# Issuing the first weight load ahead of the entry barrier, in a decode-attention kernel

## The chip, the cores and the metric

The kernel runs on one core of one Trainium2 chip. Time is device microseconds (us) of one execution; a result is the median of several executions. A profile (trace) of one execution comes with each kernel. Its "span" runs from the first to the last instruction. The engines go by the profile's short names: here PE runs the matmuls, DVE and ACT the copies, casts and activations, POOL (GpSimd) the fills of constants, and SP (SyncE) issues the large loads. A DMA is a transfer between device memory and the core's own; the profile counts 16 DMA engines.

## The reference, cut to what matters

Two attention blocks, A and B, each decode one token. A attends to the last 2048 positions of its cache, B to all 8192. Each block projects x with wq, attends over 16 key/value heads, and projects back with wo.

```python
B, Sq, D = 1, 1, 576
Hq, Hkv, Sk, Dh = 32, 16, 8192, 128          # bf16 everywhere
q = (x @ wq).reshape(B, Sq, Hq, Dh)...
scores = einsum(q, k) * Dh ** -0.5            # k: last 2048 rows (A), all 8192 rows (B)
o = einsum(softmax(scores), v)
out = concat([o_A @ wo_A, o_B @ wo_B])
```

All bytes are used once: 102.8 MB come from HBM (device memory), 2.3 KB go back.

## The kernel before

All large loads go through one queue, issued by SyncE (called SP) in a fixed order: A's wq (2, 2 and 0.5 MB), B's wq (the same), then k, v and wo. A load into a buffer that is still in use waits on SyncE for that use to end. ACT issues the two small loads of x.

```python
def load(dst, src, writes, dma, after=()):
    add("sp", lambda sp: sp.dma_start(dst, src()), writes=writes, dma=dma, after=after)

def load_x(P):
    def go(act):
        ...
            src = bass.AP(tensor=x.tensor, offset=x.offset, ap=[[9, 64], [4, 2], [1, 5]])
            return act.dma_start(xtwo[:, P, 0:5], src)
    add("act", go, writes=[("xtwo", P)], dma="x%d" % P)
...
for P in range(2):
    x_columns(P)
    parts = [(0, 4, vslots[:, 2 * P, :], ("v", 2 * P)), (1, 4, vslots[:, 2 * P + 1, :], ("v", 2 * P + 1)),
             (2, 1, kslots[:, 3, P * WQ_U:(P + 1) * WQ_U], ("k", 3, P))]
    for k, n, view, res in parts:
        load_wq(P, k, view, n, res)
        q_part(P, k, n, view, res)
    q_finish(P)
```

The list of recorded operations is then written out, engine by engine, into a block:

```python
def emit(self):
    ...
    per = {e: [o for o in self.ops if o.eng == e] for e in self.ENGINES}
    ...
    with self.nc.Block() as block:
        @block.sync
        def _(sp):
            run("sp", sp)
        ...
```

Ahead of that block stands an entry sequence that the kernel's author did not write. GpSimd fills four constants with memsets. Then all five engines meet in a barrier: each engine executes a Drain that raises a "gather" semaphore, and waits on a "release" semaphore, which GpSimd raises when the four others and its own Drain are through.

```
GpSimd: Memset x4, Drain, wait gather >= 4, release += 4
SyncE:  Drain (gather += 1), wait release >= 1       # ACT, PE and DVE likewise
```

Of the kernel before, what the change touches and what calls it, by code (L numbers as in the profile page):

```python
# [38 lines left out]
class Program:  # L39
# [147 lines left out]
    def emit(self):  # L187
        self.number()
        self.wants()
        per = {e: [o for o in self.ops if o.eng == e] for e in self.ENGINES}  # L190

        def one(eng, op):
            ins = op.fn(eng)
            if op.value is not None:
                ins.then_inc(self.sem(op.key), op.inc)

        def plain(eng, ops):
            for op in ops:
                for key in sorted(op.left, key=str):
                    eng.wait_ge(self.sem(key), op.left[key][1])  # L200
                one(eng, op)

        def looped(eng, ops):
            waits, before = self.waits_of_loop(ops)
            for key, n in sorted(before.items(), key=str):
                eng.sem_inc(self.sem(key), n)
            body = {}
            for o in ops:
                body.setdefault(o.loop[1], o)

            def some(todo):
                for place in todo:
                    for key, (n, take) in sorted(waits.get(place, {}).items(), key=lambda w: (not w[1][1], str(w[0]))):
                        ins = eng.wait_ge(self.sem(key), n)  # L214
                        if take:
                            ins.then_inc(self.sem(key), -n)
                    one(eng, body[place])

            def parts(of, i):
                todo = sorted(p for p in body if body[p].loop[3] == of)  # L220
                while todo:
                    cond = body[todo[0]].loop[2]
                    n = next((k for k, p in enumerate(todo) if body[p].loop[2] is not cond), len(todo))
                    if cond is None:
                        some(todo[:n])
                    else:
                        with eng.If(cond(i)):
                            some(todo[:n])
                    todo = todo[n:]

            with eng.Fori(0, self.outer) as v:
                with eng.Fori(*self.rounds_of(v)) as g:
                    parts("inner", g)
                parts("outer", v)

        def run(name, eng):
            ops = per[name]
            inside = [k for k, o in enumerate(ops) if o.loop]
            if not inside:
                plain(eng, ops)  # L240
                return
            lo, hi = inside[0], inside[-1] + 1
            assert len(inside) == hi - lo
            plain(eng, ops[:lo])
            looped(eng, ops[lo:hi])
            plain(eng, ops[hi:])

        with self.nc.Block() as block:
            @block.sync
            def _(sp):  # L250
                run("sp", sp)

            @block.gpsimd
            def _(pool):
                run("pool", pool)

            @block.tensor
            def _(pe):
                run("pe", pe)

            @block.vector
            def _(dve):
                run("dve", dve)

            @block.scalar
            def _(act):
                run("act", act)
# [488 lines left out]
```

## Time and profile before

| | before |
|---|---|
| time, median of 3 (range) | 250.03 us (249.70 to 250.04) |
| span of the profiled execution | 247.7 us |
| bytes loaded | 102.8 MB, nearly all through one queue, whose packets keep the 16 DMA engines busy for 98.0% of the span |
| PE, ACT, DVE busy | 68%, 35%, 33% |

The next lines are from the profile's page of the kernel before: the span, the mean busy share of the 16 DMA engines in 40 equal slices (in tenths), the rate in GB/s of each slice, and SyncE's queue.

```profile
span 247.7 us, 7505 instructions
...
DMA  7999999999999999999999999999999999999993
GB/s 270 406 433 431 430 431 421 426 423 429 431 425 429 426 421 431 422 431 434 423 429 429 423 431 429 426 437 426 429 429 423 431 426 429 434 427 427 421 406 138
...
q1 hardware_dynamic: 7936, 102.77, 98.0%
```

By the busy share only the first and the last slice are not full. The Trainium skill, "DMA: Bandwidth & Descriptors", section Specifications, gives 435 GB/s as the fabric's ceiling; most slices move 421 to 437 GB/s, so the trace agrees. Nothing that PE, ACT or DVE does can shorten such a kernel, as long as the queue is never empty. What can shorten it is an earlier start of the queue, a shorter tail after it, or fewer bytes.

The timeline shows the start. Its columns are start, duration (both us), engine, source line, operation. An engine's name with a q (SPq, ACTq) means its sequencer, which issues the DMAs; `x2` means two instructions merged into one row.

```profile
0.24 0.10 POOL L741 MEMSET const-float32-0.0<- 128x1 f32 x1 [0.24 <-issue]
...
0.34 0.10 POOL L741 MEMSET const-uint8-127<- 128x1 uint8 x1
0.73 0.60 ACTq L344 DMA_DIRECT2D xtwo<-in_A_x_dram  x1
...
0.73 0.86 SPq L380 DMA_DIRECT2D vslots<-in_A_wq_dram  x2
```

SyncE issues nothing until 0.73 us. The trace's finer records, not all of which the timeline prints, say why. SyncE's Drain stands at 0.000 us (it opens the span). GpSimd's memsets and its Drain last until 0.49 us. SyncE's wait for the release ends at 0.67 us. The first load's issue lasts from 0.734 to 1.123 us, and the first data packet starts at 1.745 us.

The same start by windows of time (columns: window, length, busy time of five engines, granted TensorE clock, DMA share, GB/s). A packet is booked whole in the window in which it begins, so the share can exceed 1 in a short window.

```profile
0.00:1.00 1.00, 0.00 (x0) 0.00 (x0) 0.00 (x0) 0.00 (x0) 0.47 (x6) 1.00 0.00 0
1.00:2.00 1.00, 0.00 (x0) 0.00 (x0) 0.00 (x0) 0.00 (x0) 1.00 (x5) 1.00 1.03 213
2.00:3.00 1.00, 0.00 (x0) 0.00 (x0) 0.00 (x0) 0.98 (x1) 1.00 (x6) 1.00 0.24 82
```

And the end, from the chain of work that ended last (start, duration, what):

```profile
220.75 23.73 DMA vslots<-in_B_wo_dram
244.48 0.04 issue
244.52 0.71 PE ktps L646 x12
245.23 0.02 issue
245.26 0.31 DVE outsb L652
```

This wo load was issued some 24 us ahead of its landing: it stood in the queue. (It is the last but one. The last, of 144 KB, landed 0.37 us after it; "the last wo load" means the one that the chain names.) After it come a last product, a cast, and the store of the output.

### The profile page before, as it was taken

How to read it: one execution, taken by the hardware profiler on the slowest of the kernel's cores; microseconds unless marked ns; L12 is line 12 of the kernel's file. 1: busy time of each engine (PE TensorE's matmuls, PEld its weight loads, DVE VectorE, ACT ScalarE, POOL GpSimd, SP SyncE). 2: the span in 40 equal slices, each digit the busy share in tenths (PEclk: the TensorE clock that was granted, in tenths of full speed). 3: DMA queues.
4: the chain of work that ended last, by engine and by line, in shares of the span. 5: the costliest groups of instructions: out<-in, count | busy, mean ns of one | idle time of the engine just before them, and what ended most of it. 6: DMA issues, size and time to landing. Idle time of an engine off the chain costs nothing. (4 is left out here: it accounts for less than half of the span.)

```text
span 247.7 us, 7505 instructions
## 1 busy us (share of the span) xinstructions
PE 169.6 (68%) x3406; PEld 132.3 (53%) x3406; DVE 81.0 (33%) x152; ACT 87.1 (35%) x92; POOL 12.9 (5%) x49
## 2 busy tenths in 40 slices
PE   0193589994999559995999638998345144685634
PEld 0031288763877458864878428785244142584522
DVE  0001225554555017564555122655004004204000
ACT  2000047767478009786578004775200000000000
POOL 7501000000000000000000000000000000000000
PEclk9999959999799979998899955999858755557555
DMA  7999999999999999999999999999999999999993
GB/s 270 406 433 431 430 431 421 426 423 429 431 425 429 426 421 431 422 431 434 423 429 429 423 431 429 426 437 426 429 429 423 431 426 429 434 427 427 421 406 138
DMA packets 8235, 102.92 MB, mean 416 GB/s; under 512 B 1184, under 2 KB 1312, under 8 KB 2080
## 3 DMA queue, kind: packets, MB, share of 16 engines
q1 hardware_dynamic: 7936, 102.77, 98.0%
q8 instruction: 8, 0.13, 0.2%
q10 hardware_dynamic: 288, 0.00, 0.1%
q14 instruction: 3, 0.02, 0.0%
HBM read 102.76 MB, written 0.00 MB: 415 GB/s over the span
## 5 line engine op out<-in xcount | busy, mean ns | idle before, releaser
L472 ACT ACTIVATE kt<-ktps 128x1024 bf16<-128x1024 bf16 x80 | 77.9, 1021 | 54.5 <-PE ktps L466 54.4
L466 PEld LDWEIGHTS ktps<-ident,kslots 128*128 128x128 bf16 x1280 | 78.9, 103 | 27.9 <-issue 27.9
L466 PE MATMUL ktps<-ident,kslots 128*128 128x128 bf16 x1280 | 85.1, 230 | 12.4 <-PEq L214 12.4
L475 DVE COPY kt<-ktps 128x1024 bf16<-128x1024 bf16 x80 | 55.2, 691 | 53.7 <-PE ktps L466 53.6
L557 PE MATMUL opsum<-vslots,ptm 128*32 128x128 bf16 x1280 | 28.1, 262 | 28.0 <-PEq L214 23.7
L557 PEld LDWEIGHTS opsum<-vslots,ptm 128*32 128x32 bf16 x1280 | 25.3, 119 | 31.6 <-issue 31.6
L486 PE MATMUL sacc<-kt,qst 128*32 128x512 bf16 x320 | 25.3, 392 | 1.8 <-PEq L214 1.8
L566 DVE TENSOR_TENSOR diag<-opsum,rows 128x512 f32<-128x512 f32 x5 | 3.5, 691 | 55.9 <-PE opsum L557 55.9
L425 PE MATMUL opsum<-vslots,xpad 128*32 128x512 bf16 x64 | 8.2, 489 | 14.8 <-DVE xpad L410 12.1
L599 ACT ACTIVATE stat<-stat 128x1 f32<-128x1 f32 (+1 forms) x2 | 0.6, 294 | 37.2 <-DVE stat L597 37.2
L425 PEld LDWEIGHTS opsum<-vslots,xpad 128*32 128x32 bf16 x64 | 2.3, 119 | 17.6 <-issue 13.1
L457 POOL COPY qst<-qtm 128x64 bf16<-128x64 bf16 x20 | 4.5, 236 | 123.2 <-PE sacc L486 113.5
L646 PE MATMUL ktps<-kslots,opj 128*32 128x144 bf16 x184 | 6.1, 326 | 5.8 <-DMA kslots<-in_B_wo_dram 3.9
L486 PEld LDWEIGHTS sacc<-kt,qst 128*32 128x32 bf16 x320 | 5.1, 94 | 8.2 <-issue 4.4
L431 ACT ACTIVATE qrow<-opsum 128x512 bf16<-128x512 f32 x2 | 1.2, 597 | 23.1 <-PE misc L425 23.1
L523 ACT ACTIVATE psb<-sacc,stat 128x2048 bf16<-128x2048 f32 x3 | 5.9, 1967 | 8.5 <-DVE stat L517 8.5
L646 PEld LDWEIGHTS ktps<-kslots,opj 128*32 128x32 bf16 x184 | 5.2, 145 | 6.4 <-DMA kslots<-in_B_wo_dram 4.2
L425 PE MATMUL misc<-vslots,xpad 128*32 128x512 bf16 x64 | 8.2, 487 | 0.0
L630 PE MATMUL misc<-acc,pick 128*128 128x32 f32 x16 | 3.8, 404 | 3.6 <-DVE acc L624 2.9
L433 DVE CAST qrow<-misc 128x512 bf16<-128x512 f32 x2 | 1.4, 692 | 14.6 <-PE misc L425 14.6
L652 DVE CAST outsb<-ktps 128x144 bf16<-128x144 f32 x2 | 0.6, 307 | 16.0 <-PE ktps L646 16.0
L630 PEld LDWEIGHTS misc<-acc,pick 128*128 128x128 f32 x16 | 3.6, 328 | 3.8 <-DVE acc L624 3.0
(66 smaller groups left out, 62.1 us busy)
## 6 DMA issues: line engine op xcount, KB each, us to landing
kslots<-in_B_k_cache_dram SPq DMA_DIRECT2D x16, 2048.0 KB, 19.6
vslots<-in_B_v_cache_dram SPq DMA_DIRECT2D x16, 2048.0 KB, 18.4
kslots<-in_A_k_cache_dram SPq DMA_DIRECT2D x4, 2048.0 KB, 29.8
vslots<-in_A_v_cache_dram SPq DMA_DIRECT2D x4, 2048.0 KB, 23.5
vslots<-in_A_wq_dram SPq DMA_DIRECT2D x2, 2048.0 KB, 9.9
vslots<-in_B_wq_dram SPq DMA_DIRECT2D x2, 2048.0 KB, 19.6
kslots<-in_A_wo_dram SPq DMA_DIRECT2D x2, 2016.0 KB, 23.8
kslots<-in_B_wo_dram SPq DMA_DIRECT2D x1, 2016.0 KB, 31.2
```

The costliest lines, as they stand in the source:

```text
L425: ins = pe.matmul(qps[c][32 * j:32 * j + 32, :], lhsT=xpad[:, P, x, :], rhs=src[:, o:o + 512], start=(u == 0), stop=(u == WQ_UNITS - 1))
L433: add("dve", lambda dve: dve.tensor_copy(qrow[:, 512:1024], misc[:, :]), reads=[B_M], writes=[("qrow", 1)])
L457: add("pool", lambda pool: pool.tensor_copy(qst[:, s * 64:(s + 1) * 64], qtm[:, o:o + 64]), reads=[("qtm", KIND[g])], writes=[("qst", s)], ...
L466: ins = pe.matmul(ktps_bf[q][:, t * 128:(t + 1) * 128], lhsT=kslots[:, s, o:o + 128], rhs=ident[:, :], start=True, stop=True, is_transpose ...
L472: add("act", lambda act, q=q, dst=dst: act.activation(dst, ktps_bf[q], ACT.Copy), reads=[("bank", q)], writes=[("kt", u % NKT, q)], tag="e ...
L475: add("dve", lambda dve, q=q, dst=dst: dve.tensor_copy(dst, ktps_bf[q]), reads=[("bank", q)], writes=[("kt", u % NKT, q)], tag="e%d%d" % ( ...
L486: ins = pe.matmul(sacc[32 * j:32 * j + 32, 512 * half:512 * half + 512], lhsT=qst[:, s * 64 + e * 32:s * 64 + e * 32 + 32], rhs=rhs, start ...
L523: return act.activation(psb[:, :].rearrange("p (x g) -> p x g", g=2), src, ACT.Exp, bias=st(P, C_NB + k), scale=SCALE, accum_out=st(P, C_L ...
L557: ins = pe.matmul(opsum[32 * j:32 * j + 32, s * DH:(s + 1) * DH], lhsT=ptm[:, o:o + 32], rhs=vslots[:, s, b * 128:(b + 1) * 128], start=(u ...
L566: return dve.tensor_tensor(diag[:, g % 2, :, :], opsum[:, :].rearrange("p (s d) -> p d s", s=NS), m, ALU.mult)
L630: ins = pe.matmul(misc[:, 0:32], lhsT=pick[:, r, :], rhs=acc[:, d, 32 * r:32 * r + 32], start=(r == 0), stop=(r == 3))
L646: ins = pe.matmul(ktps[P][32 * j:32 * j + 32, 0:OUTW], lhsT=opj[:, P, jj:jj + 32], rhs=view[:, o:o + OUTW], start=(jj == 0), stop=(jj == H ...
```

## The change

The intent is to let the first 2 MB load start while the engines are still meeting at the barrier. It touches a buffer that nothing in the entry sequence touches, and waits for nothing.

```diff
+        first = per["sp"].pop(0)
+        assert not first.left and first.dma is not None
+        one(self.nc.sync, first)
+        lead = self.nc.cur_bb.bb.instructions
+        ins = lead.pop()
+        at = next(k for k, o in enumerate(lead) if o.engine == ins.engine and "Drain" in str(o))
+        lead.insert(at, ins)
+
         with self.nc.Block() as block:
```

The instruction is taken from the end of the entry sequence and put ahead of SyncE's Drain. No instruction and no byte is added or removed.

## The prediction

> **What bounds the kernel.** Its data transfers, almost from start to end. The page's DMA row reads 9 tenths in 38 of 40 slices, one SyncE queue holds 98% of the DMA time, and nearly all slices move 421 to 437 GB/s. The Trainium skill, "DMA: Bandwidth & Descriptors", section Specifications, gives a fabric ceiling of 435 GB/s; the trace agrees. In the packet records that queue has no stretch over 0.15 us with fewer than 12 packets in flight between 1.92 and 243.5 us. PE is busy 68%, ACT 35%, DVE 33%. The chain of waits ends with the last wo load (23.7 us, mostly queueing), then matmul 0.71 us, a cast 0.31 us, the output store. So the span is: first issue at 0.73 us, 1.0 us to the first data packet, 242 us of saturated transfer, a tail of 3.5 us.
>
> **What the change does.** It moves one instruction: SyncE's first load of A's wq (2 MB) goes ahead of SyncE's drain for the entry barrier. In the timeline the span starts with that drain at 0.00 us; SyncE waits for the others (GpSimd's four memsets, 0.24 to 0.44 us, and its drain, to 0.49 us), is released at 0.66 us, and issues its first load at 0.734 us, taking 0.389 us. The first packet starts at 1.745 us: 1.01 us after the issue began, 0.62 us after it ended. (Same page, section "Latency and other measured facts": about 0.6 us to the first byte; the trace agrees counted from the issue's end.) Nothing is added or removed; the load depends on nothing computed.
>
> **What it is worth.** The issue should begin near 0.00 us and the first packet near 1.0 us, 0.73 us earlier. The 2 MB keep the queue busy 4.9 us, and the second load is issued when the barrier opens (about 0.73 us), so no pause follows. As the queue is never empty, the 0.73 us should travel to the end whole: all of it is on the critical path.
>
> The barrier should not open later: SyncE's issue ends near 0.40 us, GpSimd's drain at 0.49 us: 0.1 us of slack. The x loads (issued at 0.73 us, landing at 10.9 us) may land as before; PE's first matmul (11.4 us) waits for them, but PE later waits for B's wq, so that is hidden.
>
> **Prediction.** 250.03 - 0.73 = 249.30; I allow 0.05 us of loss: 249.35 us, range 248.9 to 249.9. Faster by over 2%: 0.01; within 2%: 0.98; slower: 0.01. The runs of before spread over 0.34 us, half the gain.
>
> **What the profile would show if right.** SyncE's first issue near 0.0 us, before the barrier; the second near 0.73 us; first data packet near 1.0 us; the other engines' starts unchanged within 0.1 us; the page's first slice above 300 GB/s (before 270); every later load landing about 0.7 us earlier, wo's last too; the same tail; span near 247.0 us.
>
> **What would make it wrong.** (1) The first issue takes much longer, or its first packet waits for something that was ready by 1.7 us: less gain. (2) SyncE's drain waits for the transfer itself: barrier 5 us late, the second load too, slower by microseconds. (3) The clock that times the kernel starts with something that moves with the first issue: gain in the span, none in the time. (4) A pause elsewhere in the queue, set by PE's release of a slot, absorbs the head start: landings early at first, not at the end.

## The result

| | before | after |
|---|---|---|
| time, median of 5 (range) | 250.03 us (249.70 to 250.25) | 249.26 us (248.82 to 249.32) |
| ratio | | 0.9969 (95%: 0.9957 to 0.9981) |
| span of the profiled execution | 247.7 us | 247.5 us |

A ratio is the mean time of one kernel's runs over that of the other's runs of the same rounds, so it is not quite the ratio of the medians. By the means the gain is 0.79 us (249.98 to 249.19). It is a change of 0.3%, small, but its interval excludes 1.

The same lines of the page, for the changed kernel:

```profile
span 247.5 us, 7505 instructions
...
DMA  8999999999999999999999999999999999999992
GB/s 326 391 444 427 432 424 421 421 429 437 429 430 418 421 426 426 430 432 426 429 426 426 429 432 426 434 429 424 432 424 429 429 426 434 429 426 425 421 407 106
...
q1 hardware_dynamic: 7936, 102.77, 98.1%
```

The first slice moves 326 GB/s in place of 270; the middle is as it was. The timeline of the start:

```profile
0.00 1.13 SPq L388 DMA_DIRECT2D vslots<-in_A_wq_dram  x2
0.23 0.10 POOL L749 MEMSET const-float32-0.0<- 128x1 f32 x1 [0.23 <-issue]
...
0.33 0.10 POOL L749 MEMSET const-uint8-127<- 128x1 uint8 x1
...
0.79 0.61 ACTq L352 DMA_DIRECT2D xtwo<-in_A_x_dram  x1
```

The first issue starts at 0.00 us. (The 1.13 us merges two issues: the finer records have them at 0.000 and 0.793 us.) The barrier opens 0.05 us later than before. The windows show the queue's start moved up:

```profile
0.00:1.00 1.00, 0.00 (x0) 0.00 (x0) 0.00 (x0) 0.00 (x0) 0.42 (x6) 1.00 0.00 0
1.00:2.00 1.00, 0.00 (x0) 0.00 (x0) 0.00 (x0) 0.00 (x0) 1.00 (x4) 1.00 1.21 262
2.00:3.00 1.00, 0.00 (x0) 0.00 (x0) 0.00 (x0) 0.92 (x1) 1.00 (x6) 1.00 0.91 377
```

The first data packet starts at 1.002 us, 0.743 us earlier. So far all is as forecast. But the chain's end is not:

```profile
220.51 23.82 DMA vslots<-in_B_wo_dram
244.33 0.04 issue
244.38 0.71 PE ktps L654 x12
245.09 0.02 issue
245.11 0.31 DVE outsb L660
```

The last wo load lands at 244.33 us, against 244.48 us: 0.15 us earlier, not 0.74. These two profiles alone would say that four fifths of the head start were lost on the way, while the times say that all of it arrived. One of the two misleads, and the first experiments ask which.

### The profile page after: what moved, and what is told of

Read it like the earlier page. It is cut to its first block, busy times and chain, and to the rows that moved or that the text cites. A ratio compares the mean times of both kernels' runs of the same rounds, so it can differ in the third digit from the quotient of the medians.

```text
span 247.5 us, 7505 instructions
## 1 busy us (share of the span) xinstructions
PE 168.7 (68%) x3406; PEld 131.5 (53%) x3406; DVE 80.8 (33%) x152; ACT 87.2 (35%) x92; POOL 12.9 (5%) x49
```

## The experiments

Two theories stood after this.

- **Full queue.** The head start travels through a queue that is never empty, and arrives whole. The pair of profiles is unlucky.
- **Given back.** The head start is lost near the end of the queue, and the time was gained by something outside the span.

Nine runs were made, two of them repeats, all correct. Each was timed in 4 to 6 executions beside 9 to 11 executions of the kernel before on the same chip (three chips in all). "Over before" below is the difference of the means.

| run | time, median | ratio (95%) | over before |
|---|---|---|---|
| again_before | 249.93 us | 0.9995 (0.9983 to 1.0007) | -0.03 us |
| again_after | 249.26 us | 0.9971 (0.9958 to 0.9984) | -0.68 us |
| late_first | 252.86 us | 1.0120 (1.0105 to 1.0135) | +2.99 us |
| nine_ahead | 249.14 us | 0.9968 (0.9956 to 0.9980) | -0.83 us |
| late_both | 253.44 us | 1.0143 (1.0128 to 1.0157) | +3.56 us |
| x_ahead | 249.20 us | 0.9969 (0.9956 to 0.9982) | -0.75 us |
| split_plain | 250.07 us | 1.0006 (0.9993 to 1.0018) | +0.18 us |
| split_ahead | 249.73 us | 0.9992 (0.9979 to 1.0005) | -0.16 us |
| x_on_sp | 249.12 us | 0.9965 (0.9952 to 0.9979) | -0.86 us |

### again_before and again_after: the same two kernels once more

No edit. The point is to have the span of every execution, of both kernels on one chip.

> The kernel before, unchanged, run as if it were a new one: it gives the spans of its executions beside their times, which the first result lacks. Theory (the head start of 0.73 us travels through a queue that is never empty): time 250.0 us, ratio 1.000, spans near 247.7 us, so that the spans of the changed kernel are about 0.7 us shorter on average and the one profile that showed 0.14 us less was an unlucky one. Rival (the head start is given back at the end of the queue, and the time gained 0.77 us from something outside the span): time minus span stays near 2.4 us in every execution here, and near 1.8 us in the changed kernel, with spans that differ by 0.2 us only.

> The changed kernel again, on the same chip as the run above. Theory: time 249.3 us, ratio 0.997, mean span about 0.7 us below that of the unchanged kernel. Rival: time 249.3 us as well, but mean span only 0.1 to 0.3 us lower, and time minus span near 1.8 us against 2.4 us.

The mean span was 248.03 us for the kernel before (6 executions; 248.10 us over the 11 others in the same rounds) and 247.40 us for the changed kernel (5; the first result's five average 247.36 us). The spans differ by 0.6 to 0.7 us, as the times do, and time minus span is the same for both. The rival "given back" falls. The first profile of the kernel before, with 247.7 us, was shorter than nearly all of its other executions. The new profile of the same kernel ends its chain so:

```profile
221.47 23.74 DMA vslots<-in_B_wo_dram
245.21 0.04 issue
245.25 0.71 PE ktps L646 x11
245.96 0.02 issue
245.98 0.31 DVE outsb L652
```

Here the last wo load lands at 245.21 us, 0.73 us later than in the first profile of the same kernel. The packet records show what differs between executions of one kernel. From the first packet to the 102nd MB they took nearly the same time. From the 102nd MB to the last packet of the loads they did not:

| profile | first packet | to 102nd MB | to the last load packet | to the end |
|---|---|---|---|---|
| before, first profile | 1.75 us | +240.04 us | +2.66 us | +3.22 us |
| before, again_before | 1.74 us | +240.16 us | +3.21 us | +3.27 us |
| after, first profile | 1.00 us | +240.16 us | +3.15 us | +3.21 us |
| after, again_after | 1.00 us | +240.29 us | +2.97 us | +3.22 us |

The time to the last packet varies by half a microsecond from one execution to the next, as much as most of the effect under study. Only the first column differs by kernel, and it differs by 0.74 us. The spans of these profiles, paired each way, show gains from 0.14 to 0.9 us.

The last 0.8 MB only bring the difference to light; it arises much earlier. Each load reports 16 completions, one for each DMA engine, and has landed when the slowest engine is done. In all eleven traces the slowest engine fell behind the mean of the 16 by another 0.6 to 1.4 us between two loads that landed at 19 to 31 us, and more than half of its lag stayed to the end. How large it was near 140 us goes with the length of the tail (correlation 0.98). At the time of the jump the queue of kind "instruction" put its first 16 KB packet (1.0 to 1.2 us) among the loads; that it is the cause was not tested. Averaged over the 16 engines, the same wo load was done at 243.66 and 243.79 us before, and at 243.04 and 243.28 us after: earlier by 0.38 to 0.75 us in every pair.

### late_first: the same lever pulled the other way

If a start 0.73 us earlier is worth 0.73 us, a start 3.5 us later must cost 3.5 us, which is far above the noise. The edit, on the kernel before:

```diff
-        add("sp", lambda sp: sp.dma_start(dst, src()), writes=writes, dma=dma, after=after)
+        add("sp", lambda sp: sp.dma_start(dst, src()), reads=["ident"] if dma == "wq00" else (), writes=writes, dma=dma, after=after)
```

> The kernel before, with the first load made to wait until GpSimd has written the identity (about 4.2 us in the trace of before), so that the first issue starts near 4.2 us in place of 0.73 us, 3.5 us late. Theory (whatever the queue's start is late or early goes whole to the end): time 253.5 us, 3.5 us over before (3.2 to 3.8), and the last wo load lands 3.5 us later. Rival (the pipeline has room that absorbs part of a late or early start, for instance by waits of SyncE on PE): under 2.5 us over before.

The time rose by 2.99 us, between the two forecasts: a miss for the stated 3.2 to 3.8 us. The last wo load landed 3.3 us later than in the first profile of before and 2.6 us later than in the second, not 3.5. The first packet came at 5.216 us, 3.47 us late. From there to the 102nd MB it took 239.78 us, less than in any of the four profiles in the table above. Something in the start had become cheaper. The timeline of late_first shows a side effect of the edit: the x loads are still issued at once, into an empty queue.

```profile
0.74 0.61 ACTq L344 DMA_DIRECT2D xtwo<-in_A_x_dram  x1
1.38 0.62 ACTq L344 DMA_DIRECT2D xtwo<-in_B_x_dram  x1
...
4.21 0.86 SPq L380 DMA_DIRECT2D vslots<-in_A_wq_dram  x2
```

The view of the tile that x is loaded into has the time from issue to landing, for late_first:

```profile
DMA to landing us min/median/max: 2.1/2.1/2.2
```

In the kernel before the two x loads took 10.1 and 12.7 us, because their 288 tiny packets (10 bytes of data or a 4-byte semaphore write each) ran among the wq packets, from 5.4 to 13.7 us.

### late_both: is it the x packets that late_first saved?

Both x loads wait for the identity as well, so they are again issued together with the first wq load. The edit on late_first (the calls also move behind the identity's definition):

```diff
-        add("act", go, writes=[("xtwo", P)], dma="x%d" % P)
+        add("act", go, reads=["ident"], writes=[("xtwo", P)], dma="x%d" % P)
```

> As late_first, but the two x loads on ACT wait for the identity too, so that they are again issued with the first wq load and not 3.5 us ahead of it. It asks why late_first cost 2.9 us where its first packet came 3.47 us late. In late_first the x packets went through the empty queue from 2.1 to 3.2 us; in the kernel before they run from 5.3 to 14.0 us among the wq packets. Theory (x's 288 small packets, mixed with the wq packets, cost the bulk transfer some 0.4 us, and late_first saved that): about 3.5 us over before, 253.4 us, and the bulk takes as long from its first packet to its 102nd MB as in before (240.0 to 240.2 us). Rival (slack in the pipeline absorbed 0.5 us of the delay): 252.9 us as in late_first, with the bulk again 0.3 to 0.4 us shorter.

The time rose by 3.56 us, the first packet came 3.49 us late, and the bulk took 240.24 us from first packet to 102nd MB, as in before. The x loads took as long as ever to land:

```profile
DMA to landing us min/median/max: 10.2/11.5/12.8
```

So a late start goes whole to the end, and the shortfall of late_first was the x packets. Mixed with the wq packets, they lengthen the bulk by 0.26 to 0.51 us (the four profiles above against 239.78 us; 0.46 us from late_both; nine_ahead and x_ahead below, with 240.01 and 240.31 us, widen this to 0.22 to 0.53 us). All of these rest on the one profile of late_first. The mean times of late_first and late_both differ by 0.60 us; no execution of one reaches the range of the other (252.78 to 253.10 and 253.43 to 253.70 us), though the intervals of the ratios, from two chips, just overlap.

The records also show where the two part. Counted from the first packet, the 1st MB had come after 3.40 us in late_first and 3.43 in late_both, the 4th after 10.41 and 10.86 us, and this 0.45 us stays to the 102nd MB. The x packets of late_both ran from 3.6 to 12.0 us of the same count. From the 15th to the 102nd MB every one of the eleven traces took 203.56 to 203.66 us: apart from the tail, what differs between these kernels lies in the first 15 MB.

### nine_ahead: does the barrier itself matter?

All nine loads that wait for nothing go ahead of SyncE's Drain. The barrier then opens very late, for all engines.

```diff
-        first = per["sp"].pop(0)
+        for _ in range(9):
+            first = per["sp"].pop(0)
             ... (the rest of the moved block, indented)
```

> All nine loads that wait for nothing (both wq, three of A's k) are issued ahead of SyncE's drain, so the barrier opens only after some 4 to 5 us and every other engine starts that much later; x lands later, PE's first matmul starts near 15 us in place of 11.3 us. Theory (only the time of the first issue counts, the barrier and the other engines' starts are off the path): time 249.3 us as with one load ahead, within 0.3 us. Rival (a late barrier costs: the x loads and PE's first products are near the path): 250.0 us or more, up to 4 us over the changed kernel.

The barrier opened at 5.5 us, as the GpSimd and ACT lines of its timeline show, and PE's first matmul started at 13.91 us (near 15 was expected), 2.6 us later than in the changed kernel:

```profile
5.54 0.20 POOL L362 MEMSET ident<- 128x128 bf16 x1 [5.10 <-POOLq L750]
5.54 0.61 ACTq L353 DMA_DIRECT2D xtwo<-in_A_x_dram  x1
```

The time was 249.14 us (mean 249.08, against 249.24 for again_after): no worse. A barrier 4.8 us later costs nothing here. Of the two, only the time of the first issue counts. The 0.16 us by which the mean is lower is not clear of the noise.

### x_ahead: can the x packets be sent through first?

The experiments pointed at up to 0.5 us more, if x could pass ahead of wq without delaying wq. The edit moves both of ACT's x loads ahead of ACT's Drain, in the changed kernel:

```diff
-        first = per["sp"].pop(0)
+        for name, eng, n in (("sp", self.nc.sync, 1), ("act", self.nc.scalar, 2)):
+            for _ in range(n):
+                first = per[name].pop(0)
                 ... (the same block, with eng in place of self.nc.sync)
```

> The changed kernel with both x loads issued by ACT ahead of its own drain as well (ACT reaches it at 0.13 us). If the x packets then get through before the wq packets fill the engines, as in late_first, the time falls by 0.3 to 0.4 us below the changed kernel, to 248.9 us, and x lands before 5 us. If they queue behind wq as before (the wq issue still starts first, at 0.00 us), x lands near 10 us and the time stays at 249.2 us, within 0.15 us. A later barrier (ACT's two issues end near 1.4 us, so it opens near 1.6 us) should cost nothing in either case; the rival, that the barrier or the second wq load matters, gives 249.6 us or more.

ACT issued x at 0.13 us in place of 0.79 us, yet the x packets started at 4.67 us (4.78 us in the changed kernel) and landed 10.0 and 12.6 us after their issue. They queued behind wq as before. The time stayed at 249.20 us, and the second wq load, issued at 2.06 us behind the later barrier, cost nothing: the first load's 2 MB still covered it.

### split_plain and split_ahead: how large must the early load be?

The strict form of the theory says that the early load must keep the queue busy until the next one arrives. The first load is cut into 128 KB and the rest. split_plain is the kernel before with the cut, split_ahead the changed kernel with the cut, so that only the 128 KB go ahead.

```diff
+        cut = 512 if (P, k) == (0, 0) else 0
+        if cut:
+            load(dst[:, 0:cut], lambda: rows_(lo, lo + cut), ["wqcut"], "wqcut")
-        load(dst, ..., [res], "wq%d%d" % (P, k))
+        load(dst[:, cut:], lambda: rows_(lo + cut, lo + n * WQ_U), [res], "wq%d%d" % (P, k))
```

> Control for the next run: the kernel before, with the first wq load cut in two, 128 KB (512 of 8192 columns) and the rest, both issued after the barrier. 102.77 MB as before in one load more. Expected 250.0 us within 0.3 us, by theory and rival alike; whatever it differs from before is the price of the cut.

> The changed kernel, but only the 128 KB piece goes ahead of the barrier; the rest of the first load is issued when the barrier opens, near 0.79 us. At 427 GB/s 128 KB are 0.3 us of work for the queue, less than the 0.73 us of head start. Theory in its strict form (the head start counts only as far as the load issued ahead keeps the queue busy): 0.3 us below split_plain and 0.45 us above the changed kernel, 249.7 us, with a stretch of idle queue near 1.5 to 1.9 us. Rival (what counts is that the first access comes early: the slow start of the first packets is paid ahead of time): 0.6 us or more below split_plain, as good as the changed kernel.

split_ahead's median was the forecast 249.73 us, and its mean was 0.34 us below split_plain's. Their intervals overlap, so the times alone do not settle it. The packets do: in split_ahead the first packet came at 1.005 us, and then, from 1.61 to 2.09 us, 5.5 packets on average were in flight, where 15.8 were in the changed kernel. Windows of split_ahead:

```profile
1.00:1.60 0.60, 0.00 (x0) 0.00 (x0) 0.00 (x0) 0.00 (x0) 0.60 (x3) 1.00 0.74 196
1.60:2.10 0.50, 0.00 (x0) 0.00 (x0) 0.00 (x0) 0.00 (x0) 0.50 (x3) 1.00 2.30 395
```

and of the changed kernel:

```profile
1.00:1.60 0.60, 0.00 (x0) 0.00 (x0) 0.00 (x0) 0.00 (x0) 0.60 (x3) 1.00 1.93 410
1.60:2.10 0.50, 0.00 (x0) 0.00 (x0) 0.00 (x0) 0.02 (x1) 0.50 (x3) 1.00 0.11 33
```

Remember that a packet is booked where it begins (the second window of the changed kernel is low because its 16 KB packets, begun before, were still under way), so look at what began first: in the first 0.6 us only half as much work began with the small piece, although it began at the same time. The first 9.44 MB (as much as all of wq) had come at 25.18 us, against 24.55 and 24.69 us in the two profiles of the changed kernel and 25.52 us in split_plain. About half of the head start was lost in the pause. The control is not perfect: in split_plain A's x landed 2.3 us after its issue (before: 10.1 us), as the small piece let it through. One of split_plain's six executions, at 250.79 us, also lifts its mean.

### x_on_sp: is it the second queue that makes x dear?

SyncE issues x in its own queue, behind the first wq load, in place of ACT's queue.

```diff
-            return act.dma_start(xtwo[:, P, 0:5], src)
-    add("act", go, ...)
+            return eng.dma_start(xtwo[:, P, 0:5], src)
+    add("sp", go, ...)
...
-        first = per["sp"].pop(0)
+        first = per["sp"].pop(2)
```

> The changed kernel with the two x loads issued by SyncE, in its own queue right behind the first wq load, in place of ACT's queue. late_first (x alone in an empty queue) against late_both (x among the wq packets) put the price of mixing at about 0.5 us. If that price comes from two queues taking turns packet by packet on the same engines, x in the same queue saves up to 0.4 us: 248.8 to 248.9 us, and the bulk from first packet to 102nd MB near 239.8 us. If it is the price of 288 small packets wherever they stand in a busy engine's work, the time stays at 249.2 us, within 0.15 us. In both cases x lands near 6 to 7 us, right behind the first 2 MB, and PE starts sooner, which the theory of the full queue says is worth nothing.

The time was 249.12 us (mean 0.86 us under before; the changed kernel had 0.68 and 0.79), and the bulk took 240.18 us: no saving beyond the noise. The Trainium skill, "DMA: Bandwidth & Descriptors", section "Rules for kernel authors", says that spreading DMAs over the issuing engines gains no bandwidth; here the reverse, bringing them together, gained none either. So the second queue is not what makes x dear. x landed at 7.8 and 8.0 us (6 to 7 were expected), and PE's first matmul started at 8.38 us in place of 11.34 us. Three microseconds earlier at the start of PE were worth nothing that these runs can see.

## Why the prediction was right

- **The bound: right.** In the two profiles each of before and after, no stretch over 0.15 us has fewer than 12 packets in flight from 0.25 us after the first packet to the 102nd MB, and from the 15th MB on the rate is the same in all kernels (the 203.6 us above). One slip: the page's 98% is the share of the span in which the queue's packets keep the 16 engines busy, not, as the prediction has it, the queue's share of the DMA time, which is higher still.
- **The worth of the move, 0.73 us, all of it on the path: right.** The first packet came 0.743 us earlier; the means fell by 0.79 and 0.68 us. The intervals (0.5 to 1.1 us for the first result) do not fix it better. late_both fixes the slope better: 3.49 us late at the first packet, 3.56 us later in time (3.2 to 3.9 by its interval).
- **Loss of 0.05 us: not seen.** It is smaller than the noise.
- **"0.1 us of slack" at the barrier: slightly wrong.** The prediction took SyncE's Drain as short (7 ns in before). Behind the load it took 112 ns, from 0.450 us, and SyncE, not GpSimd, arrived last: the barrier opened 0.05 us later. nine_ahead shows that such a delay is free.
- **"Span near 247.0 us" and "wo's last too": wrong as a check on one profile.** The forecast subtracted 0.73 us from a span of 247.7 us that was itself some 0.4 us short of the kernel's mean. The changed kernel's mean span is 247.4 us. The difference of means, 0.6 to 0.7 us, is what was meant.
- **The ways to be wrong.** (1) and (2) did not occur: the issue took 0.386 us, and the Drain, over at 0.56 us, did not wait for the transfer, which landed at 7.7 us. (3) is excluded by time minus span. (4) is excluded by the packets: a head start absorbed on the way would show between the 15th and the 102nd MB, where all traces agree within 0.1 us.

What stays open is why 288 tiny packets cost the bulk 0.2 to 0.5 us, when their own recorded durations add up to 2.6 us over 16 engines, 0.16 us each. In late_both against late_first, up to the 15th MB, these 0.16 us and wq packets that ran longer, by 0.29 us an engine in sum, make up the 0.45 us; the gaps between packets are the same. Why the wq packets ran longer is not shown. Why the slowest engine's lag differs from one execution to the next is open too. No run beat the changed kernel by more than the noise.

## What to carry to other kernels

When one queue is full from its first packet to its last, the moment of its first issue is a term of the total by itself: moving it by some time moves the end by the same time, while a later barrier or a later start of the compute engines costs nothing (here up to 4.8 and 2.6 us were tried). The load that goes ahead must be long enough to cover the queue until the next one arrives. For effects of a few tenths of a percent, compare means of many executions, and compare profiles by the bytes that have come, or by the mean over the DMA engines; the landing of a whole load waits for the slowest engine, and in a single profile it can be off by as much as the effect.

## What the Trainium skill lacked or had wrong

- "DMA: Bandwidth & Descriptors", Specifications and "Latency and other measured facts": the first byte after about 0.6 us agrees if it is counted from the end of the issue instruction (0.62 to 0.64 us in the eleven profiles); from its start it is 1.00 to 1.02 us, as the issue itself takes 0.39 us. The page does not say from where it counts.
- The same page gives a fixed cost of about 2.0 us to a DMA (section "Anatomy of one DMA", for GpSimd's path) and puts most of it at the completion. It has nothing on a slow start of the packets: here the first 2.1 MB took 6.0 to 6.2 us from the first packet, in before and after, and the 2.1 MB loads behind wq 4.9 us each. The first sixteen packets, of 16 KB each, took 1.2 us (median), later ones 0.61 us.
- No page gives what tiny packets cost the large ones beside them in a full queue. The same page's section "Bandwidth" has about 10.5 ns a packet for a small load by itself, issued from GpSimd. Here x's packets took 8.9 ns each in the mean, 0.16 us on each engine; the runs show 0.2 to 0.5 us on a 240 us transfer.
- "VectorE: DVE Perf Modes", section "The DRAIN you can't avoid", puts the Drains that the runtime adds before and after a program at about 12 ns, constant, on all engines. It does not cover the Drain of the program's own entry barrier, which is not constant: it took 7 ns on SyncE with nothing ahead of it, 112 ns behind one load, 372 ns behind nine, 396 ns on ACT behind two loads, and 188 ns on GpSimd behind its memsets.
- "Runtime: NRT & Kernel Launch" describes the barriers that the runtime adds around a program; no page that was read has the one that the program itself carries at its entry. Here it held SyncE's first issue back by 0.73 us.
